# Cutting the PV bursts among dense matmuls from halves of sixteen into quarters of eight

## The chip, the cores and the metric

One core of a Trainium2 chip runs the whole kernel. The metric is the device time of one execution in microseconds (us), the median of several runs.

Words used below: a **dense step** is four projection matmuls of 512 moving columns, one on each 64x64 quarter of the TensorE array. A matmul's weights are its `lhsT`, its moving columns those of its `rhs`. **PV** is the product of attention probabilities with V, a **burst** a group of PV matmuls between two dense steps. An **interval** is the time from the start of one matmul to the start of the next on the same quarter. An **eviction** is the read of a finished PSUM tile by another engine; a PSUM **bank** is here one of the four tiles that dense steps fill. DVE is VectorE, ACT is ScalarE, PE is TensorE and PEld its weight loads. In the profile's lines `PT` holds the probabilities, `po` the PV result, `q_ps` the banks, `qz` and `kt` the evicted q and k, and `seen` takes one-column reads that only keep an order.

## The reference, cut to what matters

Two attention blocks over the same x (2048 rows, 1024 columns, 32 heads of 32) are mixed by a gate. The change touches only block B: every position attends to 8 positions, two apart.

```
def _B_ref(x, wqkv, wo):                 # cut
    W, dil = 8, 2
    idx = pos[:, None] - off[None, :]    # off = 0, 2, .. 14
    logits = einsum("bhsd,bhswd->bhsw", q, k[idx]) * scale ; masked softmax
    o = einsum("bhsw,bhswd->bhsd", attn, v[idx])
    return o.reshape(B, S, D) @ wo
out = g * A_ref(x, ...) + (1 - g) * B_ref(x, ...)
```

## The kernel before

Even and odd rows form two independent sequences of 1024, handled as 18 blocks of 56 to 64 queries against 64 keys. Heads go four at a time, so there are eight column groups `c`. In each, 64 dense steps compute q and k of the *next* work, and the small matmuls of the five batches (four blocks each, two in the fifth) are put in among them at fixed step numbers.

The dense steps, 32 for each half of a column group, fill four PSUM banks. Steps 0 to 7 and 16 to 23 write the k banks, 8 to 15 and 24 to 31 the q banks:

```
def step(slot, kt):
    for j in range(2):
        for r in range(2):
            o = (slot + 2 * r) % 4
            mm(o, r, kt, j, slot < 2)
    if kt == KT - 1:
        ...  # slots 0, 1: one-column reads "seen" order the two row halves
        if slot >= 2:
            ...  # slot 2: ACT copies k; slot 3: ACT and DVE evict q, two reads each
```

The scores, PV and the schedule (cut):

```
def scores(g):
    s2b = ps_s.tile([P, 2, 2, 256], F32, name="s2b", tag="s")
    ...  # 16 matmuls; then ACT: exp into PT[g % 2]; DVE: times mask

def pv(g, only):
    for s_ in only:
        for i in range(4):                 # heads
            for dm in range(2):            # two blocks
                for par in range(2):       # even, odd rows
                    ...
                    nc.tensor.matmul(o2[64 * h:64 * h + w, par, s_, i, :], lhsT=pt[r, i, o:o + w],
                                     rhs=V[r, m, 4 * c + i, :], start=True, stop=True)
    if only[-1] < ns - 1:
        return
    ...  # DVE: two reciprocals and two multiplies evict po (one PSUM tile for all batches)

for g, (c, m, n) in enumerate(BATCHES):
    p_ = 64 * c + ((43, 55, 75, 86, 97) if c < KT - 1 else (43, 55, 75, 83, 92))[m // 4]
    events.append((p_, lambda g=g: scores(g)))
    at = p_ + (14 if c < KT - 1 or m < 8 else 12)
    apart = 2 if c < KT - 1 or m < 8 else 0
    for k in range(n // 2):
        events.append((at + apart * k, lambda g=g, k=k: pv(g, (k,))))
```

DVE and ACT run in the order in which the program names their work.

The softmax here doesn't subtract the row's maximum and nothing guards it: scores larger than these inputs give would overflow.

## Time and profile before

| | before |
|---|---|
| median | 472.67 us (3 runs, 472.12 to 472.69) |
| profiled span | 470.1 us |
| TensorE busy | 99% |
| attention stage (line L421, first to last start) | 140.3 us |
| PV matmuls | 1152: 68 bursts of 16 and two of 32 |

The length of the stage is read from the view of line L421; the columns are line, engine, operation, tiles, count, then durations in ns, then first and last start in us.

```profile
L421 PE MATMUL q_ps<-xT,WkB x1024: 374/376/400, 215.6 to 338.8; 64*64 64x512 bf16 x171
...
L421 PE MATMUL q_ps<-WqA,xT x256: 374/376/392, 340.9 to 355.9; 64*64 64x512 bf16 x128
```

On DVE's timeline the eviction of q is

```profile
253.98 1.41 DVE L461 TENSOR_SCALAR qz<-q_ps,qsel 128x512 bf16<-128x512 f32 x2
```

and on PE's timeline the next dense steps that write the same banks are

```profile
255.75 0.89 PE L421 MATMUL q_ps<-xT,WqB 64*64 64x512 bf16 x12
```

The eviction ends at 253.98 + 1.41 = 255.39, the bank is needed at 255.75: 0.36 us are spare. In the other half of each column group only some 0.07 us are (same reading: from the end of DVE's q eviction to the start of step 8). The k banks are closer still in every second half: ACT's copy of k ends some 0.03 us before step 0 of the next column group starts, before the change and after it.

### The profile page before, as it was taken

To read this page: it belongs to the slowest core of one execution; us is meant where nothing else is said; L and a number is where in the kernel's file an instruction comes from. 1 tells how busy PE (TensorE), PEld (TensorE's weight loads), DVE (VectorE), ACT (ScalarE), POOL (GpSimd) and SP (SyncE) were. 2 spreads that over 40 slices of the span, in tenths; PEclk is the share of its full clock that TensorE was granted. 3 is DMA by queue.
4 is the path that set the end of the run, shared out by engine and by line. 5 is a ranking of instruction groups with operands and counts; after the bars stand their busy time and mean duration, and the time that the engine had idled before them with its cause. 6 is when DMAs were issued, how large, how long until landed. Compare 5 with 4: busy or idle time off the path is not lost.

```text
span 470.1 us, 13202 instructions
## 1 busy us (share of the span) xinstructions
PE 466.2 (99%) x5762; PEld 265.9 (57%) x5762; DVE 278.1 (59%) x612; ACT 169.6 (36%) x277; POOL 15.7 (3%) x30
## 2 busy tenths in 40 slices
PE   8999999999999999999999999999999999999997
PEld 5444444445444444444888888888764444444444
DVE  2586689990219999999566676667660049800000
ACT  1443311112433333335465555555543134221121
POOL 2500001400000000000000000000000000000000
PEclk9999999999999999999999999999999999999999
DMA  9999960000653233627326523533763923221111
GB/s 235 201 244 371 349 212 0 0 1 1 226 130 117 83 141 123 162 93 251 105 55 106 116 59 73 88 80 82 92 165 76 216 75 79 68 56 45 34 33 46
DMA packets 98188, 55.14 MB, mean 117 GB/s; under 512 B 69074, under 2 KB 90578, under 8 KB 98130
## 3 DMA queue, kind: packets, MB, share of 16 engines
q1 hardware_dynamic: 92818, 49.61, 41.3%
q10 hardware_dynamic: 5312, 4.69, 3.1%
q8 instruction: 45, 0.74, 0.7%
q14 instruction: 13, 0.11, 0.1%
HBM read 26.10 MB, written 15.86 MB: 89 GB/s over the span
## 4 chain that ended last, share of the span: by engine, by line
PE 99%; DMA 1%; DVE 0%; issue 0%; DVEq 0%
PE q_ps L421 26%; PE d_ps L627 12%; PE p_ps L325 12%; PE pk_ps L196 12%; PE g_ps L264 12%; PE e_ps L627 12%; PE p_ps L361 9%; PE po L501 2%; PE s2b L479 2%; DMA xrow<-in_A_x_dram 1%; PE kv_ps L284 0%; PE w_ps L180 0%; PE xt_ps L210 0%; DVE osb L634 0%; DVE xT L211 0%
## 5 line engine op out<-in xcount | busy, mean ns | idle before, releaser
L421 PE MATMUL q_ps<-xT,WqB 64*64 64x512 bf16 x1024 | 70.2, 376 | 0.0
L421 PE MATMUL q_ps<-xT,WkB 64*64 64x512 bf16 x1024 | 69.8, 376 | 0.0
L171 DVE TENSOR_SCALAR e<-e 128x512 f32<-128x512 f32 x64 | 27.2, 424 | 62.0 <-ACT e L170 61.9
L325 PE MATMUL p_ps<-WvB,xT 128*128 128x512 bf16 x256 | 57.4, 379 | 0.0
L196 PE MATMUL pk_ps<-WkA,xT 128*128 128x512 bf16 x256 | 55.6, 379 | 0.3 <-DVE xT L211 0.3
L264 PE MATMUL g_ps<-pk,xrow 128*128 128x512 bf16 x256 | 55.4, 379 | 0.0
L484 ACT ACTIVATE PT<-s2b 128x928 bf16<-128x928 f32 (+4 forms) x40 | 34.2, 855 | 50.2 <-PE s2b L479 49.2
L486 DVE TENSOR_TENSOR PT<-PT,mask 128x928 bf16<-128x928 bf16 (+4 forms) x40 | 23.6, 589 | 36.5 <-ACT PT L484 36.5
L421 PEld LDWEIGHTS <-WkB 64*64 64x64 bf16 x1024 | 39.7, 107 | 7.3 <-DMA vd<-tmp 0.2
L361 PE MATMUL p_ps<-WqA,xT 128*128 128x512 bf16 x192 | 43.4, 379 | 0.0
L627 PEld LDWEIGHTS <-pqT 128*128 128x128 bf16 x272 | 26.0, 98 | 29.6 <-issue 0.2
L627 PEld LDWEIGHTS <-OBT 128*128 128x128 bf16 x272 | 26.0, 98 | 29.4
L264 PEld LDWEIGHTS <-xrow 128*128 128x128 bf16 x256 | 25.0, 98 | 30.2
L421 PEld LDWEIGHTS <-WqB 64*64 64x64 bf16 x1024 | 38.6, 107 | 6.1 <-DVE qz L461 0.2
L196 PEld LDWEIGHTS <-xT 128*128 128x128 bf16 x256 | 24.8, 98 | 30.3 <-DVE xT L211 0.8
L325 PEld LDWEIGHTS <-xT 128*128 128x128 bf16 x256 | 24.9, 98 | 30.2 <-issue 0.5
L634 DVE TENSOR_SCALAR osb<-e_ps,omg 128x128 bf16<-128x128 f32 x1 | 0.4, 351 | 57.3 <-PE e_ps L627 57.3
L330 ACT CAST tmp<-p_ps 128x512 bf16<-128x512 f32 x32 | 18.7, 587 | 37.9 <-PE p_ps L325 32.5
L501 PEld LDWEIGHTS <-PT 64*56 64x56 bf16 (+2 forms) x1152 | 29.1, 104 | 5.5
L170 ACT ACTIVATE e<-pk_ps 128x512 f32<-128x512 f32 x32 | 18.9, 597 | 36.2 <-PE pk_ps L196 32.5
L361 PEld LDWEIGHTS <-xT 128*128 128x128 bf16 x192 | 18.8, 98 | 22.7
L627 PE MATMUL d_ps<-WoA,pqT 128*128 128x512 bf16 (+1 forms) x136 | 30.9, 370 | 0.0
(71 smaller groups left out, 542.1 us busy)
## 6 DMA issues: line engine op xcount, KB each, us to landing
vd<-tmp SPq DMA_DIRECT2D x16, 264.0 KB
out_dram<-osb ACTq DMA_DIRECT2D x31, 128.0 KB
xrow<-in_A_x_dram SPq DMA_DIRECT2D x3, 1024.0 KB
pqd<-tmp SPq DMA_DIRECT2D x12, 256.0 KB
WvA<-in_A_wqkv_dram SPq DMA_DIRECT2D x2, 1024.0 KB
WoA<-in_A_wo_dram SPq DMA_DIRECT2D x2, 1024.0 KB
WvB<-in_B_wqkv_dram SPq DMA_DIRECT2D x2, 1024.0 KB
WqA<-in_A_wqkv_dram SPq DMA_DIRECT2D x2, 1024.0 KB
```

The costliest lines, as they stand in the source:

```text
L170: nc.scalar.activation(out=e[:], in_=pj[:], func=ACT.Exp)
L171: nc.vector.tensor_scalar(out=e[:], in0=e[:], scalar1=1.0, scalar2=1e-6, op0=ALU.min, op1=ALU.add)
L196: nc.tensor.matmul(pj[:], lhsT=xT[:, kt, t * P:(t + 1) * P], rhs=WkA[half][:, kt, :], start=(kt == 0), stop=(kt == KT - 1))
L264: nc.tensor.matmul(pj[:], lhsT=xrow[:, t, kt * P:(kt + 1) * P], rhs=pk[:, t, half * 512:(half + 1) * 512], start=(t == 0), stop=(t == NB - 1))
L325: nc.tensor.matmul(st["pj"][:], lhsT=xT[:, kt, t * P:(t + 1) * P], rhs=WvB[half][:, kt, :], start=(kt == 0), stop=(kt == KT - 1))
L330: nc.scalar.copy(out=v[:, half * 16:(half + 1) * 16, 0:Dh], in_=st["pj"][:].rearrange("p (h e) -> p h e", h=16))
L361: nc.tensor.matmul(st["pj"][:], lhsT=xT[:, kt, t * P:(t + 1) * P], rhs=WqA[half][:, kt, :], start=(kt == 0), stop=(kt == KT - 1))
L421: nc.tensor.matmul(banks[o][64 * j:64 * j + 64, :], lhsT=lhsT(r, kt, j), rhs=rhs(r, kt), start=first and kt == 0, stop=kt == KT - 1, skip_ ...
L484: nc.scalar.activation(out=pt[:, :, 0:W_], in_=s2b[:].rearrange("p a b s -> p (a b) s")[:, :, 0:W_], func=ACT.Exp, scale=SCALE)
L486: nc.vector.tensor_tensor(out=pt[:, :, 0:W_], in0=pt[:, :, 0:W_], in1=mask[:, None, base:base + W_].broadcast_to([P, 4, W_]), op=ALU.mult)
L501: nc.tensor.matmul(o2[64 * h:64 * h + w, par, s_, i, :], lhsT=pt[r, i, o:o + w], rhs=V[r, m, 4 * c + i, :], start=True, stop=True)
L627: nc.tensor.matmul(st["ps"][:, 0:n], lhsT=lhsT, rhs=W[c0 // 512][:, c, c0 % 512:c0 % 512 + n], start=(side == 0 and c == 0), stop=(side == ...
```

## The change

The intent: bursts of eight with a dense step between them, in the hope that dense matmuls cover more of the weight loads that PV needs. Nothing is added or removed.

```
-            def pv(g, only):
+            def pv(g, only, heads=range(4)):
-                    for i in range(4):
+                    for i in heads:
-                if only[-1] < ns - 1:
+                if only[-1] < ns - 1 or heads[-1] < 3:
                     return
-                    events.append((at + apart * k, lambda g=g, k=k: pv(g, (k,))))
+                    for i in range(2 if apart else 1):
+                        events.append((at + apart * k + i, lambda g=g, k=k, h=range(2 * i, 2 * i + 2) if apart else range(4):
+                                       pv(g, (k,), h)))
```

## The prediction

> **What bounds the kernel now.** I read the page first: shares of the engines, then the chain that ended last, then the groups of the attention stage.
>
> ```profile
> span 470.1 us, 13202 instructions
> ...
> PE 466.2 (99%) x5762; PEld 265.9 (57%) x5762; DVE 278.1 (59%) x612; ACT 169.6 (36%) x277; POOL 15.7 (3%) x30
> ...
> PE 99%; DMA 1%; DVE 0%; issue 0%; DVEq 0%
> ```
>
> TensorE is busy all the time, and 99% of the chain that sets the end is TensorE's own work. PE can only become faster if the same matmuls are issued closer together, so the question is how far apart they are, not who waits for whom. The view of the PV line (L501) and the score line (L479) shows the small matmuls that lie among the dense projection matmuls of L421:
>
> ```profile
> L501 PEld LDWEIGHTS <-PT x1152: 99/104/110, 228.1 to 350.9; 64*57 64x57 bf16 x97, 64*56 64x56 bf16 x79, 64*64 64x64 bf16 x16
> L501 PE MATMUL po<-V,PT x1152: 173/177/200, 228.3 to 350.9; 64*57 64x33 bf16 x90, 64*56 64x33 bf16 x85, 64*64 64x33 bf16 x17
> ```
>
> These durations are latencies of overlapping instructions; the cost has to be read from starts. The timeline of PE gives it, first where only dense steps run, then around one batch's two PV bursts:
>
> ```profile
> 217.34 1.90 PE L421 MATMUL q_ps<-xT,WqB 64*64 64x512 bf16 x32
> 219.07 1.90 PE L421 MATMUL q_ps<-xT,WkB 64*64 64x512 bf16 x32
> ```
>
> ```profile
> 254.64 0.30 PE L501 MATMUL po<-V,PT 64*57 64x33 bf16 x11
> 254.76 0.38 PE L421 MATMUL q_ps<-xT,WkB 64*64 64x512 bf16 x1
> 254.76 0.23 PE L501 MATMUL po<-V,PT 64*57 64x33 bf16 x5
> 254.82 0.62 PE L421 MATMUL q_ps<-xT,WkB 64*64 64x512 bf16 x7
> 255.20 0.30 PE L501 MATMUL po<-V,PT 64*57 64x33 bf16 x12
> 255.32 0.38 PE L421 MATMUL q_ps<-xT,WkB 64*64 64x512 bf16 x1
> ```
>
> Columns: start, duration, engine, line, shapes, count. 32 dense matmuls (8 steps of four, one on each 64x64 quarter of the array) start 1.73 us before the next 32, so a dense step takes 1.73 / 8 = 0.216 us. The first PV matmul of a burst starts at 254.64 and the first dense one after it, on the same quarter, at 254.76: a burst costs 0.12 us. The next burst starts 0.56 us after the first, which is two dense steps (0.43) and one burst (0.12 to 0.13). Sixteen matmuls on four quarters are four on each, so one PV matmul takes 0.12 / 4 = about 0.029 us of its quarter.
>
> Check by the sum of the stage. L421 runs from 215.6 to 355.9, 140.3 us. 2304 / 4 = 576 dense steps x 0.216 = 124.4; 1152 / 16 = 72 bursts x 0.12 = 8.6; the scores, 576 / 4 = 144 rounds at some 0.049 (dense restart after a score burst, 225.10 less 224.90, over 4) = 7.1. Together 140.1, so there is almost no waiting in this stage: about 0.2 us.
>
> **What the Trainium skill says.** "TensorE: Matmul & The Clock Gate", section Back-to-back issue gap, gives N/2.4 + 2.5 ns for a warm matmul and a floor near 25 ns for small ones. The dense steps agree (512 columns: 216 ns). For PV with 33 columns the streaming part would be 16 ns; the trace shows 29, so streaming isn't the limit. The same page, section LDWEIGHTS, puts a weight load at P/1.2 ns, 47 ns for 56 columns. Here the trace differs: successive PV matmuls of one quarter, each with new weights, come every 29 ns, so the measurement decides. "TensorEngine Tiling (Array Packing)", section Tiling Modes, Key Properties, says tiles run LdWeights and Matmul independently, and that a change of the tiling mode drains the array. All three kinds here are on 64x64 quarters, so no drain should come with more alternation, and the trace agrees: the step before the PV burst of 255.20 isn't longer than another.
>
> **The change, part by part.** It removes and adds no instruction. 67 of the 72 bursts are cut in two (seven column groups with 9 bursts, 63, and the first two batches of the last group, 4); the other five stay. Each of the 67 becomes eight matmuls, a dense step, eight matmuls.
>
> (a) Matmul time. On one quarter the order was dense, PV, PV, PV, PV, dense, dense; it becomes dense, PV, PV, dense, PV, PV, dense. A dense matmul of 0.216 us hides the weight load of whatever follows it; a PV matmul doesn't, so each PV matmul is followed by one interval of a weight load, whoever comes next. Four intervals stay four: 0.12 us both ways. The only difference is the kind of weights loaded: one interval per cut that loaded 56 or 57 PV columns now loads 64 dense ones. If the interval scales with columns, 29 x 7/57 is 3 to 4 ns at most; 67 x 3.5 ns = +0.2 us. My estimate is +0.1.
>
> (b) The release of the output tile. All batches share the one PSUM tile po. The last PV quarter now starts one dense step later, 0.22 us, so its eviction (two reciprocals, two multiplies) may end later and the next batch's first PV matmul may have to wait. The tightest ordinary case is the batch above, on DVE:
>
> ```profile
> 255.74 0.41 DVE L486 TENSOR_TENSOR PT<-PT,mask 128x452 bf16<-128x452 bf16 x1 [0.34 <-ACT PT L484]
> 256.05 0.27 DVE L512 RECIPROCAL rd<-po 128x8 f32<-128x8 f32 x2
> 256.29 0.76 DVE L514 TENSOR_TENSOR Ob<-po,rd 128x256 bf16<-128x256 f32 x2
> ```
>
> The eviction ends at 256.29 + 0.76 = 257.05, the next batch's PV starts at 257.47: 0.42 us spare. Its start at 256.05 is set by the masking ahead of it in DVE's order and not by PV, whose last matmul ends at about 255.55. With PV at 255.77 the eviction doesn't move at all. I went through the 35 batches that have a successor in columns 0 to 6 in the same way: spare time is 0.4 to 0.8 us in four kinds of batch and 3.0 in the fifth; where PV itself releases the eviction (0.07 us after its end) there are 3.0. In the short batch of two blocks the one-column reads "seen" now come ahead of the eviction and may push it 0.3 us, out of 0.83 spare. So no wait: 0.
>
> (c) The other side: the tail of a PV burst no longer stands as one block, and the next scores come at the same dense step as before. Nothing is gained there, since ACT and DVE aren't on the chain.
>
> Sum: +0.1 us on 472.67, so 472.8.
>
> **Rivals.**
> Rival 1, what the change probably hopes for: dense matmuls cover more weight loads, so that bursts get cheaper. For it: each burst costs 29 ns per matmul where streaming needs 16; against it: the interval from the last PV to the dense one is as long as the others, as weights for a quarter can only be loaded once the matmul before has begun. If the first PV of each quarter were free and that last interval too, 67 x 0.029 = 1.9 us would be saved (470.8); if all 67 fell to the streaming time, 67 x 4 x 0.013 = 3.5 us (469.2). Even this is 0.7%, not 2%.
> Rival 2, the output tile becomes a wait: if the evictions ended a dense step later and there were no spare time, up to 32 batches x 0.22 = 7 us (1.5%, 479.7). The spare times speak against it; it would take semaphore delays of 0.4 us that the trace doesn't show.
> Rival 3, alternation itself costs something: if each of 67 new passages from dense to PV and back took some 20 ns more (skew between quarters, late instructions), +1.3 us (474.0). One PV burst near 333.7 took 0.2 us longer with no wait named, so such stalls exist, but one in 72.
>
> **Range and chances.** The timing runs before lie within 0.6 us. Rival 1 in part and rival 3 in part bound the range: 471.8 to 474.0. More than 2% is 9.5 us, which exceeds the whole cost of the bursts, 8.6, on the fast side, and the full rival 2 on the slow one. Faster 0.01, same 0.98, slower 0.01.
>
> **What would show it.** In the changed trace: a burst of eight costs 0.057 to 0.062 us between its first PV and the dense matmul after it (right), or 0.03 (rival 1), or 0.08 (rival 3). L421's stretch stays 140.3 us within 0.4. DVE's first reciprocal in the batch type shown starts no later against the following PV, and no wait of PE for L514 appears (else rival 2). I am wrong if the stretch moves by over 1 us, or if the time changes outside it, where nothing was touched.

## The result, and the profile after

| | before | after |
|---|---|---|
| median of 6 runs each | 472.45 us (472.12 to 472.69) | 472.69 us (472.12 to 472.80) |
| ratio after / before | | 1.0003, 95% interval 0.9990 to 1.0016 |
| profiled span | 470.1 us | 471.0 us |
| attention stage | 140.34 us | 140.31 us |

A ratio is the mean time of one kernel's fast runs over that of the other's of the same rounds, so it is not quite the ratio of the medians quoted. The two kernels take the same time.

The profiled spans differ by 0.9 us, but not through the change: the view of L421 in the changed kernel starts later by the same amount.

```profile
L421 PE MATMUL q_ps<-xT,WkB x1024: 374/376/400, 216.5 to 339.6; 64*64 64x512 bf16 x171
...
L421 PE MATMUL q_ps<-WqA,xT x256: 373/376/398, 341.8 to 356.8; 64*64 64x512 bf16 x128
```

Ahead of that start both kernels are the same, and over all thirteen profiles the start lies anywhere between 215.5 and 216.5 us. That is spread of the first phase. The stage itself is what the change can move.

PE's timeline of the same batch as in the prediction, now in quarters:

```profile
255.53 0.21 PE L501 MATMUL po<-V,PT 64*57 64x33 bf16 x2
255.59 0.38 PE L421 MATMUL q_ps<-xT,WkB 64*64 64x512 bf16 x1
255.60 0.22 PE L501 MATMUL po<-V,PT 64*57 64x33 bf16 x6
255.66 0.40 PE L421 MATMUL q_ps<-xT,WkB 64*64 64x512 bf16 x3
255.81 0.21 PE L501 MATMUL po<-V,PT 64*57 64x33 bf16 x2
255.87 0.38 PE L421 MATMUL q_ps<-xT,WkB 64*64 64x512 bf16 x1
...
256.64 0.90 PE L421 MATMUL q_ps<-xT,WqB 64*64 64x512 bf16 x12
```

From the first PV matmul (255.53) to the first dense one on the same quarter (255.59) it is 0.06 us, where a burst of sixteen took 0.12. One dense step with one burst takes 255.81 - 255.53 = 0.28 us, where two dense steps with one burst took 0.56. Twice as many bursts of half the cost: nothing is gained.

To a finer scale I took, for each dense step, the mean of its four starting times, and from the distance of neighbouring steps the 215.6 ns of a dense step alone. A burst of sixteen adds 116.4 ns (68 bursts, without one halt told below), a burst of eight 60.3 ns (134 bursts), so a cut costs 2 x 60.3 - 116.4 = 4.2 ns, 67 of them 0.28 us. A dense step behind a burst takes 219.2 ns even where no burst follows it, and there are 40 of those instead of 70, which gives back some 0.11 us. The stage doesn't show the remainder as a loss because the profile of before holds a single unexplained halt of 0.20 us within a PV burst near 333.7; without it, that stage is 140.14 us and the changed one 0.17 us longer, 2.5 ns per cut.

The start of every single matmul in the packed trace tells where these nanoseconds lie. The PV intervals of a quarter are the same before and after, 28 to 30 ns in the mean (a table follows with the narrower weights). But after a dense matmul that stands behind PV the next one on its quarter starts 219 ns later, after any other dense matmul 216 ns. A cut puts one more dense matmul behind PV, at 3 to 4 ns.

DVE's timeline around the same batch after the change:

```profile
255.07 1.40 DVE L461 TENSOR_SCALAR qz<-q_ps,qsel 128x512 bf16<-128x512 f32 x2
256.63 0.40 DVE L486 TENSOR_TENSOR PT<-PT,mask 128x452 bf16<-128x452 bf16 x1 [0.17 <-ACT PT L484]
256.95 0.27 DVE L512 RECIPROCAL rd<-po 128x8 f32<-128x8 f32 x2
257.18 0.75 DVE L514 TENSOR_TENSOR Ob<-po,rd 128x256 bf16<-128x256 f32 x2
```

Less the 0.89 us by which this batch's first PV comes later in this profile (255.53 - 254.64), the eviction of po starts where it did (256.95 - 0.89 = 256.06; 256.05 before). But the eviction of q ahead of it has moved: it ends at 255.07 + 1.40 = 256.47, and its bank is needed at 256.64. Of 0.36 us spare, 0.17 are left. The change took half of a reserve that the prediction had not counted.

### The profile page after: what moved, and what is told of

Same layout as the page of the kernel before. It is cut to its first block, busy times and chain, and to the rows that moved or that the text cites. A ratio compares the mean times of both kernels' runs of the same rounds, so it can differ in the third digit from the quotient of the medians.

```text
span 471.0 us, 13171 instructions
## 1 busy us (share of the span) xinstructions
PE 465.2 (99%) x5732; PEld 266.7 (57%) x5762; DVE 278.2 (59%) x612; ACT 169.6 (36%) x277; POOL 15.5 (3%) x30
## 4 chain that ended last, share of the span: by engine, by line
PE 95%; DVE 2%; DMA 1%; issue 1%; SPq 0%; ACT 0%; DVEq 0%; ACTq 0%
PE q_ps L421 26%; PE d_ps L629 12%; PE g_ps L264 12%; PE e_ps L629 11%; PE pk_ps L196 11%; PE p_ps L325 10%; PE p_ps L361 8%; PE po L501 2%; PE s2b L479 2%; DMA WkA<-in_A_wqkv_dram 1%; DVE tmp L172 1%; DVE tmp L342 1%; PE kv_ps L284 0%; DVE e L171 0%; PE w_ps L180 0%
## 5 line engine op out<-in xcount | busy, mean ns | idle before, releaser
L421 PE MATMUL q_ps<-xT,WqB 64*64 64x512 bf16 x1024 | 69.9, 377 | 0.0
L421 PE MATMUL q_ps<-xT,WkB 64*64 64x512 bf16 x1024 | 69.4, 377 | 0.0
L421 PEld LDWEIGHTS <-WkB 64*64 64x64 bf16 x1024 | 42.0, 107 | 7.1 <-DMA vd<-tmp 0.2
L421 PEld LDWEIGHTS <-WqB 64*64 64x64 bf16 x1024 | 40.3, 107 | 5.1 <-DVE qz L461 0.2
L501 PEld LDWEIGHTS <-PT 64*56 64x56 bf16 (+2 forms) x1152 | 37.9, 105 | 6.6
L501 PE MATMUL po<-V,PT 64*56 64x33 bf16 (+2 forms) x1152 | 37.7, 177 | 0.0
```

The costliest lines, as they stand in the source:

```text
L421: nc.tensor.matmul(banks[o][64 * j:64 * j + 64, :], lhsT=lhsT(r, kt, j), rhs=rhs(r, kt), start=first and kt == 0, stop=kt == KT - 1, skip_ ...
```

## The experiments

Theory: each PV matmul costs its quarter one interval in which the next weights are loaded, wherever the bursts are cut. Rival 1: a dense matmul hides a load per burst, so cuts matter. Rival 2: the wait for po. Rival 3: alternation costs by itself. A second question came up on the way: what waits lie closest below the surface.

### One burst per batch

```
-                apart = 2 if c < KT - 1 or m < 8 else 0
+                apart = 0
```
(in the kernel before)

> The kernel before, with the two halves of every batch of four blocks put into one burst of 32 (eight PV matmuls per quarter of the array between two dense ones). Theory: every PV matmul costs one weight load of about 29 ns on its quarter, however the bursts are cut, so a burst of 32 costs about 0.235 us, twice a burst of 16, and the time stays within 0.4 us of before. Rival 1 (the dense matmul hides one load per burst, so that fewer bursts hide fewer): 32 merged bursts x 0.029 us = +0.9 us, and a burst of 32 costs over 0.26 us.

Measured: 472.63 us against 472.11 before, ratio 1.0008 (0.9993 to 1.0023). The stage is 140.62 us, 0.28 longer than before's and 0.48 longer than before's without its halt, 15 ns for each of the 32 merged pairs. A burst of 32 adds 243 ns to its dense step, 30.4 per PV matmul of a quarter, where halves add 29.1 and quarters 30.15. Rival 1 wanted over 0.26 us and 29 ns per merged pair; it falls, but merging isn't free either. My own figure of twice a half (233) was 10 ns too low. The dense step behind the burst is longer too, 228 ns instead of 219. Why is open.

### Single heads where there is room

```
+                    parts = 1 if not apart else 4 if m in (4, 16) else 2
+                    for i in range(parts):
+                        step = apart // 2 * k * parts + i
+                        ...  # pv of heads 4 * i // parts to 4 * (i + 1) // parts at at + step
```
(in place of the two quarters of the changed kernel)

> The changed kernel, with the batches that have room (the second and the fifth of each column group) cut further, into single heads: one PV matmul per quarter between dense steps. Theory: a dense step with one PV round takes 216 + 30 to 33 ns, half of what a pair adds (60 ns) or 1 to 3 ns more; no wait; the time within 0.5 us of before. Rival 1: a lone PV matmul has its load hidden by the dense one ahead and adds only its streaming, 16 ns. Rival 3 (alternation costs by itself): 216 + over 40 ns.

Measured once only: 473.32 us (state unknown), the stage 141.61 us, 1.3 longer than in the changed kernel. A dense step with one PV round takes 247.5 ns in the median, 32 over a plain one. So not even a lone PV matmul between two dense ones has its load hidden for nothing: rival 1 wanted 16. But "no wait" was wrong: the mean is 250, and in seven column groups one step is 75 to 86 ns too long, 0.55 of the 1.3 us. On DVE's timeline

```profile
235.15 0.76 DVE L514 TENSOR_TENSOR Ob<-po,rd 128x256 bf16<-128x256 f32 x2
235.83 0.41 DVE L433 COPY seen<-q_ps 128x1 f32<-128x1 f32 x2
```

the one-column reads end at 235.83 + 0.41 = 236.24, having stood behind the later eviction of po, and on PE's timeline the dense step that must follow them starts only then:

```profile
236.29 0.41 PE L421 MATMUL q_ps<-xT,WqB 64*64 64x512 bf16 x4
```

That is the first sign that lateness of PV is passed on through DVE's order of work.

### Narrower weights, in halves and in quarters

```
-   nc.tensor.matmul(o2[64 * h:64 * h + w, par, s_, i, :], lhsT=pt[r, i, o:o + w],
+   nc.tensor.matmul(o2[64 * h:64 * h + 34, par, s_, i, :], lhsT=pt[r, i, o:o + 34],
```
(results wrong; once in the kernel before, once in the changed one)

> Wrong results on purpose: the kernel before (halves), with each PV matmul taking 34 columns of weights instead of 56, 57 or 64. Theory (the interval between PV matmuls of one quarter is the load of the next weights[...]): PV after PV goes from 29 to about 19 ns, three of the four intervals of a burst shrink, the fourth (dense weights, 64 columns) stays: a burst costs about 0.090 instead of 0.117 us, 72 x 0.027 = -2 us. With a floor of 25 ns per matmul: -0.8 us. If the load isn't what sets it: 0.

> Wrong results on purpose: the changed kernel (quarters), with 34 columns of weights in each PV matmul. Theory: in a pair only one of the two intervals shrinks, the other still loads 64 dense columns: a burst of eight costs about 0.050 instead of 0.060 us; 134 x 0.010 = -1.4 us against the changed kernel, and some 0.6 to 0.9 us more than the same narrow matmuls in halves: cutting now costs, since it swaps a load of 34 columns for one of 64. Rival (no difference between the kinds of interval): both narrow kernels take the same time.

Measured: 471.04 us for halves, 471.86 for quarters, against 472.27 for the kernel before (ratios 0.9977, 0.9962 to 0.9992, and 0.9989, 0.9974 to 1.0003). PE's timeline of the halves, one burst:

```profile
252.00 0.27 PE L501 MATMUL po<-V,PT 64*34 64x33 bf16 x11
252.11 0.38 PE L421 MATMUL q_ps<-xT,WqB 64*64 64x512 bf16 x1
```

A burst now adds 104.3 ns in the mean, 12 less than with full weights, not the 27 that I expected. A burst of eight adds 56.4 ns, 4 less. The stage is 139.39 us in halves, 0.75 shorter than before's without its halt, which is the size that the expectation named for a floor of 25 ns. In quarters it is 139.93 us (139.79 without a halt of 0.14 us near 273.3), so 0.4 us more than in halves. The medians of the two narrow kernels are too close for their spread; these readings are from one profile each.

So far this fits the theory that the load of the next weights sets an interval. The intervals one by one don't. In quarters, on the quarter of the array that starts first (PE's and PEld's lines of the timeline):

```profile
252.14 0.20 PE L501 MATMUL po<-V,PT 64*34 64x33 bf16 x2
252.14 0.09 PEld L501 LDWEIGHTS <-PT 64*34 64x34 bf16 x1
252.17 0.10 PEld L421 LDWEIGHTS <-WqB 64*64 64x64 bf16 x1
252.19 0.38 PE L421 MATMUL q_ps<-xT,WqB 64*64 64x512 bf16 x1
```

The two PV matmuls start at 252.142 and 252.170 in the packed trace, the dense one at 252.195: 28 ns while 34 columns are loaded, then 25 ns while 64 are. The means over the bursts behind a plain dense step whose starts can be put on quarters without doubt (24 to 43 of each kernel), in ns:

| | first interval | those between | last (loads dense weights) |
|---|---|---|---|
| before | 28.5 | 29.1, 29.1 | 29.9 |
| changed | 28.3 | | 29.2 |
| narrow halves | 28.0 | 25.3, 25.1 | 25.5 |
| narrow quarters | 28.3 | | 25.1 |

Narrow PV weights shorten every interval of a burst but the first, and the last as much as the others, though 64 columns are loaded in it either way. So the length depends on the width of the PV weights (or of their output, which goes with it), but not on that of the weights that are being loaded. What sets it stays open, and so does whether 25 ns is a floor, since only one narrower width was run. No run kept the weights from one PV matmul to the next either: that the load fills the interval is argued from its place, not shown.

### Fewer moving columns

```
-   rhs=V[r, m, 4 * c + i, :]
+   rhs=V[r, m, 4 * c + i, 0:8]        # and the output cut to 0:8
```
(in the changed kernel; results wrong)

> Wrong results on purpose: the changed kernel with 8 moving columns in each PV matmul instead of 33. Theory (loads of weights set the interval): nothing changes, within 0.4 us of the changed kernel, a burst of eight costs 0.060 us. Rival (streaming sets it): 25 columns fewer, 10 ns per matmul, 288 x 0.010 = -3 us.

Measured: 471.95 us, ratio to before 0.9992 (0.9975 to 1.0008); the stage is 140.32 us and a burst of eight adds 60.3 ns, the very figures of the changed kernel. With a quarter of the moving columns nothing changes. Streaming doesn't set the interval.

### No PV at all

```
-   nc.tensor.matmul(o2[64 * h:64 * h + w, par, s_, i, :], lhsT=..., rhs=V[...], start=True, stop=True)
```
(in the kernel before; results wrong)

> Wrong results on purpose: the kernel before without its PV matmuls; the evictions of po, the transfers and the order stay. Theory (all of PV lies on the path, 72 bursts x 0.117 us): -8.4 us, 464.1. Rival (part of the time of PV only fills waits that would be there anyway): clearly less than 8 us saved. It is also the most that any placement of PV could save.

Measured: 467.63 us, ratio 0.9903 (0.9888 to 0.9918): 4.6 us saved, not 8.4. The table of waits for the attention stage of this run names what took the rest (who waited for whom: total us, times, longest):

```profile
PEld L421 <- DVE qz L461: 6.7, 16, 0.5
PEld L421 <- issue: 2.5, 8, 0.3
```

Without PV the dense steps reach the q banks before DVE has evicted them, sixteen times, once per half of a column group. Totals of the weight-load row overstate the loss on the path; the dense steps are longer than normal by 3.96 us in all, at steps 7, 8, 39 and 40 (q banks, 2.3 us) and at 63 and 0 (k banks, whose copy stands behind an exp on ACT, 1.7 us). PV itself adds 8.4 us (68 bursts x 116.4 ns and two of 32 x 243 ns), and 8.4 - 3.96 = 4.4; the stage is 4.5 us shorter.

This was a story until tested. So the same kernel without PV got evictions that read half of their columns:

```
+   nc.gpsimd.memset(qz[:, part, par, 256:512], 0.0)
-   nc.vector.tensor_scalar(out=qz[:, part, par, :], in0=ps[:], ...)
+   nc.vector.tensor_scalar(out=qz[:, part, par, 0:256], in0=ps[:, 0:256], ...)
    # likewise ACT's copy of k
```

> Wrong results on purpose: the kernel without PV (467.6 where 464.1 was expected), with the evictions that free the q banks made shorter: DVE's q evictions and ACT's k copies read 256 of 512 columns, GpSimd fills the rest with zeros. Theory: without PV the dense steps come so fast that they wait for those banks (3.96 us of excess in the trace, in the steps around 0, 8 and 40 of each column group), so the rest of PV's 8.4 us comes out now: about 464, and those waits are gone. Rival (PV costs only 4.6 us of the path, the rest is a change of pace of the dense steps themselves): stays near 467.6.

Measured: 463.82 us, ratio 0.9824 (0.9806 to 0.9841), and in its table of waits

```profile
PEld L421 <- DVE qz L463: 1.3, 7, 0.2
```

The stage is 131.69 us, 8.65 shorter than before's: 8.4 plus the halt of 0.2. (The seven waits that are left on the weight-load row don't lengthen their dense steps. Two other steps of seven column groups are some 20 ns too long each, 0.3 us in all; about as much came off with the longer dense steps behind the 70 bursts of before, so the sum still closes.) So PV's whole cost of 8.4 us is on the path, but a faster PV alone could have brought home only 4.6 of it; the rest would have become a wait for the banks.

The control is the changed kernel with the same short reads:

> Wrong results on purpose, the control: the changed kernel with the same shorter q and k evictions. Theory: the changed kernel waits for none of them, so nothing comes of it: within 0.4 us of the changed kernel. Rival (the changed kernel already loses time to those banks): it gets 0.5 us or more faster.

Measured: 472.68 us, ratio 1.0007 (0.9993 to 1.0022), the stage 140.26 us. The changed kernel loses at most 0.05 us to these banks. (The output passed the comparison although half of q and k were zeros, and so did that of the last run with short reads below; neither is the reference's computation.)

### Quarters further apart

```
-   events.append((at + apart * k + i, lambda ...
+   events.append((at + 2 * (apart * k + i), lambda ...
```

> The changed kernel with two dense steps between the quarters instead of one, so the last quarter of a batch comes three steps (0.65 us) later than in the changed kernel, four later than before. Theory of the spare time: about 0.4 to 0.5 us are spare before the next batch needs po, so this goes over by 0 to 0.2 us in three of five batches: PE waits of 0.1 to 0.2 us appear ahead of the first PV of some batches, +1 to +3 us in all (473.5 to 475.5). Rival (the eviction is never near the path): 0 within 0.4 us.

Measured: 480.80 us, ratio 1.0183 (1.0168 to 1.0198), +8.6 us, where I had expected 1 to 3. DVE's timeline in this run:

```profile
247.15 0.76 DVE L514 TENSOR_TENSOR Ob<-po,rd 128x256 bf16<-128x256 f32 x2
247.82 1.40 DVE L461 TENSOR_SCALAR qz<-q_ps,qsel 128x512 bf16<-128x512 f32 x2
```

and PE's:

```profile
247.96 0.24 PE L501 MATMUL po<-V,PT 64*56 64x33 bf16 x8
...
248.74 0.38 PE L421 MATMUL q_ps<-xT,WqB 64*64 64x512 bf16 x1
249.28 0.41 PE L421 MATMUL q_ps<-xT,WqB 64*64 64x512 bf16 x3 [0.17 <-DVE qz L461]
```

Both waits are there. The eviction of po ends at 247.91, and the next batch's PV starts 0.05 us later, at 247.96, as it does in three of the five batches of each group: that is the wait that I had foreseen. The q eviction has been pushed behind it and ends at 247.82 + 1.40 = 249.22; the dense step that needs that bank stands still after the first of its four matmuls, from 248.74 to 249.28. This second wait is the larger one. To test that, the q evictions were shortened as above:

> Wrong results on purpose: the kernel with quarters two dense steps apart (+8.6 us), with DVE's q evictions reading 256 of 512 columns and GpSimd filling the rest. Theory: most of its loss (about 0.75 us per column group) is the wait of the dense matmuls for the q banks, whose eviction now stands behind the late eviction of po in DVE's order; the wait for po itself is only some 0.3 to 0.5 us per group. So the loss falls from 8.6 to between 2 and 4 us. Rival (the loss is the wait for po, as the prediction had it): stays at 7 to 8 us.

Measured: 474.67 us, ratio 1.0054 (1.0039 to 1.0069). The stage falls from 148.90 to 143.11 us; against the 140.31 of the changed kernel the loss falls from 8.6 to 2.8 us, and no wait for q is left in the table of waits. So two thirds of the loss was the q banks. The remainder is of the size that I had given to po, and the trace has it there: 2.4 us in the dense steps with the first PV of those three batches, each 0.05 us behind the eviction of po, and 0.35 us in one halt at 280.0, where that eviction had waited for an outgoing transfer.

A last dose, three dense steps apart, failed as an experiment:

> The same with three dense steps between the quarters: the last quarter comes seven steps (1.5 us) later than in the kernel before, and its eviction falls behind the evictions of q or the masking of the next batch in DVE's order. Theory of the spare time: waits of 1 to 2 us in three of five batches of each column group, +20 to +40 us in all. Rival (the order on DVE absorbs it): under +5 us.

Measured: 529.13 us and, not intended, a wrong result (relative error 0.24). With this spacing the last quarter of the third batch comes at step 98, after the fifth batch's scores at 97, whose exp writes the same one of the two PT tiles; the fourth batch is overtaken likewise (109 after 107). So the run multiplied the wrong probabilities and waited for them as well. Its 57 us are no measure of the spare time, and I draw nothing from them.

## Why the prediction was right

Time and range: 472.8 was predicted (471.8 to 474.0), 472.69 measured, against 472.45 for the kernel before in the same comparison.

**Step (a)**, four intervals stay four, held. A burst of eight takes 0.06 us on the timeline, as foretold, and bursts of one, two, four and eight rounds all cost 29 to 32 ns per PV matmul. That a dense matmul hides the load behind it is in the trace too: 96% of the loads' records in the stage start within 2 ns after a matmul does, in plain dense steps the one before on the same quarter, and a PV matmul follows a dense one after 216 ns, as another dense one would. The sum of +0.1 to +0.2 us came out (0.17 in the stage, below the spread of the medians), but by luck: the reason given, one load per cut of 64 columns instead of 57, isn't what the trace shows. The last interval before a dense matmul is no longer after the cut than before it (29.2 and 29.9 ns), and in narrow quarters it takes 25 ns with 64 columns. The 3 to 4 ns of a cut lie in the dense matmul behind PV.

**Rival 1** was rightly rejected, but its upper bound (all PV falling to 16 ns of streaming, 3.5 us) lies beyond anything measured: the shortest intervals of any run were about 25 ns, which would give 67 x 4 x 4 ns = 1.1 us.

**Step (b)**, no wait appears, held, and the eviction of the batch shown kept its place. That of the third batch of each group didn't: there PV now releases it (0.06 us after its end, 0.25 before), and the time to spare before the next PV fell from 0.58 to 0.38 us; in the fifth it fell from 0.83 to 0.50, as foreseen. The premise that po with 0.42 us spare is the tightest place was wrong. The q banks were tighter, 0.07 us in one half and 0.36 in the other, and the change cut the 0.36 to 0.17. The prediction looked only for who reads the tile that PV writes, not for whose work stands behind that reader on DVE. That one dense step of delay was small enough for a reserve nobody had counted is luck; the next doubling cost 8.6 us, mainly there.

**Rival 2**, the wait for po, didn't appear at this dose, and made up about a third of the loss with the quarters two steps apart.

**Rival 3**, a cost of alternation, was right in kind and too large in size: 3 to 4 ns per passage instead of some 20, 2.5 net of all.

What stays open: what sets the length of an interval, why the dense matmul behind a burst takes longer, and most of all behind a burst of 32, and what the single halts are of which I found one in the profile of before (0.20 us) and one in that of the narrow quarters (0.14 us), with no wait named.

## What to carry to other kernels

The small matmuls with new weights cost one interval apiece here, 25 to 32 ns, in bursts of any length; splitting and spreading them hid none of it. So before cutting bursts compare the cost per matmul in short and long bursts that the trace already holds. Before moving work later, follow its reader's queue: the reserve that is used up first may belong to the next work on that engine. And an ablation that saves less than the sum of what was removed points at the wait that lies next below: relieve it in the same experiment, and see whether the sum closes.

## What the Trainium skill lacked or had wrong

- "TensorE: Matmul & The Clock Gate", section LDWEIGHTS, gives P/1.2 ns, 47 ns for 56 columns. On a 64x64 quarter, PV matmuls with fresh weights of 56 or 57 columns follow each other every 29 ns, and the interval doesn't go with the columns that are loaded in it (28 ns with 34 of them, 25 ns with 64, in narrow quarters).
- The same page, section Back-to-back issue gap, has a floor near 25 ns for small matmuls; the narrow runs agree (25 ns in all intervals of a burst but the first). The formula that the prediction takes from it stands there for an isolated matmul; here dense matmuls with fresh weights keep it on each quarter (216 ns). The section doesn't say that this floor also holds for each quarter by itself when four work side by side.
- The same page, Part 3, "What overlaps and what doesn't", says that matmuls start strictly in program order. Here a dense matmul starts at 255.59 and six PV matmuls that stand ahead of it in the program at 255.60 and after, evidently on other quarters (the trace doesn't name the quarter). No run here tested this further.
- No page says how a burst of small matmuls bears on the dense one behind it: here a dense step took 219 ns behind bursts of four to sixteen and 228 behind bursts of 32, instead of 216.
